# Unequal column tiles in the output product of a convolution and SwiGLU kernel: 384 + 384 and twice 256 + 128 columns

## Chip, cores and metric

The kernel runs on one core of a Trainium2 chip. The metric is the device time of one execution in microseconds (us). All data is float32.

## What is computed

The reference is a lightweight convolution (softmax over seven taps per head, eight heads), followed by RMS normalisation and a SwiGLU feed-forward block:

```
x: (8, 4096, 192)  ->  causal convolution over 7 positions, per head  ->  (32768, 192)
xn  = x / sqrt(mean(x*x) + 1e-6) * rms_g
g   = xn @ w_gate          # 192 x 1536
val = xn @ w_val           # 192 x 1536
out = (g * sigmoid(g) * val) @ w_out      # 1536 x 192, out: (32768, 192)
```

## The kernel before

The 32768 tokens are worked through in 32 pairs of two groups of T = 512 tokens. The first pair runs through a start-up code of its own (`plain`, `outer`); the other 31 are objects of the class `Pair`. For each pair TensorE runs two stages, one after the other:

1. the gate and value products (line L754): 120 matrix products of 64 contraction rows by 512 tokens, by a scheme with fewer products than the plain one, whose sums and differences are made by VectorE, ScalarE and GpSimd;
2. the output product (line L884): hidden values times `w_out`. It too is done by a scheme with seven products of half size in place of eight. The table `OUTS` lists them: each entry has a form (which sum of hidden values, which sum of weights), one of three PSUM banks X, Y, Z in which it accumulates, and a range of steps k. Over a pair that makes 42 steps.

One step multiplies a hidden tile `src` (128 hidden rows by 512 tokens) with 96 columns of weights, `right` (128 hidden rows by three blocks of 32 features). The weights are the stationary operand and the tokens are the moving one, so the result lies with features on partitions and tokens along the row: 96 features by 512 tokens. TensorE is used as four column tiles of 32 columns (`tile_position=(0, 32 i)`), and tile i writes the PSUM partitions 32 i to 32 i + 31. The 96 x 512 results fill 128 partitions by 384 columns of a bank. Before the change all four tiles do the same amount in two products each:

- columns 0 to 255 (`wide`): tiles 0 and 1 have feature block 0, tiles 2 and 3 have block 1; the 32-token blocks go alternately to the even and the odd tile of the two;
- columns 256 to 383 (`slim`): all four tiles have feature block 2, and every fourth 32-token block each.

So a step is eight products, four of 256 columns and then four of 128. `Pair.products` is a generator: it yields after each product of stage 1 and after each half of a step. The order of all other engines' work is a list written out by hand (`ORDER`), where a word like `p2` means that TensorE's generator is taken two yields further, and the other words name an operation and its engine (V VectorE, A ScalarE, G GpSimd, D a DMA). The waits between engines follow from the data.

When a bank is complete, VectorE (L899) transposes it in blocks of 32 x 32 into the output tile `o_sb`, whose partitions are then tokens. There are two output tiles per pair, one per group of 512 tokens, in a pool of two buffers. Each is stored by the words `Dst0-` and `Dst1-` early in the next pair (L957): three DMAs per group before the change, each with runs of 64 features (256 bytes) per token. The DMAs are issued by the sync engine's queue (SP), in the order of the list: the stores of group 0, the loads of the convolution's input xh for a later pair, the stores of group 1, the writes of the normalised activations to a buffer xd in DRAM, and at the end of the pair the loads of xb, the next pair's moving operand, from xd (words `DfetA` and `DfetB`, four DMAs of 384 KB, L659). In the last pair there is no next pair: the stores of group 1 come as soon as its sums are done, those of group 0 end the program, and the middle feature block's stores (c == 1) are issued by ScalarE's queue.

Constants: `P` = 128, `Q` = 32, `NQ` = 4, `HP` = 64, `NM` = 3, so `NM * P` = 384.

Of the kernel before, what the change touches and what calls it, by code (L numbers as in the profile page):

```python
# [19 lines left out]
def kernel(  # L20
# [11 lines left out]
    P = nc.NUM_PARTITIONS  # L32
# [10 lines left out]
    T = 512  # L43
# [3 lines left out]
    HP = P // 2  # L47
    KP = D // HP
    Q = 32
    NQ = P // Q  # L50
# [7 lines left out]
    LOW, UPP = slice(0, HP), slice(HP, P)  # L58
# [178 lines left out]
    def load_out(i):  # L237
# [28 lines left out]
        out=taps[:], in0=w_sb[:], in1=stat[:].to_broadcast([P, H, K]), op=ALU.subtract  # L266
# [7 lines left out]
        out=taps[:], in0=taps[:], in1=ssum[:].to_broadcast([P, H, K]), op=ALU.mult  # L274
# [153 lines left out]
    def part_tap(p, k, j):  # L428
# [4 lines left out]
        if k == 0:  # L433
            h = SIDE[j]
            acc[p, j] = h, pick(h, False)
# [11 lines left out]
        if k == K - 1:  # L447
            h, i = acc.pop((p, j))
            free[h].append(i)
            ended[p] = ended.get(p, 0) + 1  # L450
            if ended[p] == len(SIDE):
                x_sb.pop(p)
# [229 lines left out]
    def pick(h, full):  # L682

        i = next((i for i in free[h] if ((h, i) in whole) == full), free[h][0])
        free[h].remove(i)
        return i
# [5 lines left out]
    def put(at, do):  # L692
        heapq.heappush(line, (at, next(tick), do))
# [10 lines left out]
    def copy(eng, dst, src, s=1):  # L704
        if eng == "A":
            nc.scalar.activation(out=dst, in_=src, func=AF.Copy, scale=float(s))  # L706
        elif s < 0:
            nc.vector.tensor_scalar(out=dst, in0=src, scalar1=-1.0, scalar2=None, op0=ALU.mult)
        else:
            nc.vector.tensor_copy(out=dst, in_=src)  # L710
# [95 lines left out]
    NM = D // (2 * Q)  # L806
# [13 lines left out]
    )  # L820
    HOME = {"X": 0, "Y": 1, "Z": 1}
    SIDE = (0, 1, 0)
    RIGHT = {1: B11, 2: B21, 3: B22, 4: T4, 5: T1, 6: T2, 7: T3}

    class Pair:
# [36 lines left out]
        def products(self):  # L862
            for u, v, i in itertools.chain(*CHAINS):
                for h in range(2):
                    self.units[u].product(h, v, i)
                    yield
            for form, b, lo, hi in OUTS:
                first = form in (1, 7)
                if first:
                    self.open(b, False)  # L870
                for k in range(lo, hi):
                    src, right = self.left(form, k), RIGHT[form][:, k]
                    fresh = first and k == 0
                    wide = src.rearrange("p (b q e) -> p q b e", q=2, e=Q)
                    slim = src.rearrange("p (b q e) -> p q b e", q=NQ, e=Q)
                    for i in range(NQ):
                        self.tile(b, i, 0, 2 * P, right[:, i // 2], wide[:, i % 2], fresh)
                    yield
                    for i in range(NQ):
                        self.tile(b, i, 2 * P, P, right[:, 2], slim[:, i], False)  # L880
                    yield

        def tile(self, b, i, at, n, left, cols, fresh):
# [30 lines left out]
        def do(self, eng, name):  # L914
            act, *at = name.split(".")
            p, n = self.p, NM * P
            if name in self.past:
                return
            self.past.add(name)
            if len(at) == 2:  # L920
                self.units[int(at[1])].do(eng, act, int(at[0]))
            elif at:
                self.sum(int(act[1]), int(at[0]), eng)
            elif act == "c1":
                self.open("Y", True)
                copy(eng, self.some("Y"), self.some("X"))
            elif act in ("s7", "c2"):
                t = self.tl[act] = tiles.pop(0)
                copy(eng, t[:, 0:n], self.some("Z" if act == "s7" else "X"))
            elif act in ("C22", "C21"):  # L930
                t = self.tl["s7" if act == "C22" else "c2"][:, 0:n]
                b = "X" if act == "C22" else "Z"
                nc.vector.tensor_tensor(out=t, in0=self.some(b), in1=t, op=ALU.add)
                if b == "Z":
                    self.close(b)
                    if p == PAIRS - 1:
                        for name in ("T22", "T21", "st1"):
                            if name not in self.past:
                                self.do(eng, name)
            elif act in ("T22", "T21"):  # L940
                t = self.tl.pop("s7" if act == "T22" else "c2")
                self.turn(t, 1, int(act[2]) - 1)
                tiles.append(t)
            elif act in ("T11", "T12"):
                b = "Y" if act == "T11" else "X"
                self.turn(self.bank(b), 0, int(act[2]) - 1)
                self.close(b)
            elif act in ("st0", "st1"):
                g = int(act[2])
                r = p * PT + g * T  # L950
                o = self.o_sb.pop(g)[:].rearrange("p a d -> p (a d)")
                o = o.rearrange("p (b d) -> p b d", d=HP)
                for c, rows, lo, hi in ((0, LOW, 0, 8), (1, UPP, 0, 8), (2, slice(0, P), 8, 12)):
                    n = T // (hi - lo)
                    to = out[r : r + T, c * HP : (c + 1) * HP].rearrange("(b p) d -> p b d", p=n)
                    q = nc.scalar if c == 1 and p == PAIRS - 1 else nc.sync
                    q.dma_start(out=to, in_=o[rows, lo:hi, :])  # L957
            else:
                self.ahead(eng, act)

# [16 lines left out]
    def plain(hts):  # L977


        groups = [(u, g, f) for u in range(NU) for g in (1, 0) for f in range(NF)]  # L980
        groups[0 : 2 * NF] = [(0, g, f) for f in range(NF) for g in (1, 0)]
        held = {}

        def products():
            for u, g, f in groups:
                if len(hts) <= u:
                    hts.append(big.tile([P, 2, NF, T], F32, name="ht"))
                bks = held[u, g, f] = [free[h].pop(0) for h in range(2)]
                for k in range(KP):
                    for h in range(2):  # L990
                        nc.tensor.matmul(  # L991
                            out=bank(h, bks[h])[:], lhsT=wf[u][HALF[h], k * NF + f, :],
                            rhs=xb[HALF[h], g, k, :], start=(k == 0), stop=(k == KP - 1),
                            skip_group_check=True,
                        )
                yield

        def silus():
            for i in groups:
                sg = tiles.pop(0)  # L1000
                nc.scalar.activation(out=sg[:], in_=bank(0, held[i][0])[:], func=AF.Silu)
                held[i].append(sg)
                yield

        def values():
            for u, g, f in groups:
                *bks, sg = held.pop((u, g, f))
                nc.vector.tensor_tensor(  # L1008
                    out=hts[u][:, g, f, :], in0=bank(1, bks[1])[:], in1=sg[:], op=ALU.mult
                )  # L1010
                tiles.append(sg)
                for h in range(2):
                    free[h].append(bks[h])
                yield

        return products(), silus(), values()

    LAG = 138
# [114 lines left out]
    p, sl, v = plain(hts)  # L1133
# [31 lines left out]
    c = base + 200  # L1165
# [4 lines left out]

    for j in range(len(SIDE)):
        put(c + 240 + 700 * (j // 2), functools.partial(part_tap, 2, 0, j))
        for k in range(1, K):
            at = c + 250 + 100 * k + 50 * j if j < 2 else c + 960 + 80 * k
# [58 lines left out]
```

## Time and profile before

| | |
|---|---|
| median of 3 runs | 2621.24 us (2618.13 to 2623.8) |
| profiled execution, its own time | 2620.28 us |
| its span, first to last instruction | 2618.4 us |
| instructions | 71028 |
| TensorE busy | 2580.3 us (99%), 29002 matmul records, granted clock 0.999 |
| VectorE, ScalarE, GpSimd busy | 87%, 62%, 79% |
| DMA | 138.01 MB, mean 53 GB/s |
| instruction packets of queue q8 | 227, 3.72 MB |

How to read it: PE is TensorE's matmul side, PEld its weight loads, DVE is VectorE, ACT ScalarE, POOL GpSimd, SP the sync engine; a q behind an engine's name is its queue of instructions or DMAs. A row of a group gives the line, the engine, the operation, the result and operand by the program's names (`ps` is a PSUM bank, `ht` a hidden tile, `nt`, `early`, `more`, `tls` and `tile` are work tiles, `wo_sb` the output weights, `x` the buffer of the first input tile, which later holds sums of the weights), the shape (`128*32 128x256`: 128 contraction rows, 32 stationary columns, 256 moving columns), the count, the busy time and the mean of one, and the idle time before. An f32 product stands in the trace as two records, each with a weight load. "issue" is time in which an engine waited for nothing that the profile shows.

### The profile page before, as it was taken

The page shows a single profiled execution, that of the slowest core. Times are in us where ns is not written, and L with a number is a line of the kernel's source. Part 1 is how long each engine was busy: PE and PEld are TensorE (multiplying, and loading weights), DVE is VectorE, ACT ScalarE, POOL GpSimd, SP SyncE. Part 2 cuts the span into 40 slices and gives each one's busy share as a digit, 9 for nine tenths or more (in the row PEclk, how much of TensorE's full clock was granted, in tenths as well). Part 3 has the DMA queues.
Part 4 walks back from the last instruction along what each step waited for, and adds up shares of the span by engine and source line. Part 5 has one row for each costly group of instructions (what it writes and reads, how often), then busy time and mean ns, then how long its engine had stood idle before and what let it go on. Part 6 is the DMA issues. An engine that isn't in the chain of part 4 may idle for free.

```text
span 2618.4 us, 71028 instructions
## 1 busy us (share of the span) xinstructions
PE 2580.3 (99%) x29002; PEld 1866.1 (71%) x29002; DVE 2265.0 (87%) x3617; ACT 1617.3 (62%) x2967; POOL 2079.0 (79%) x1693
## 2 busy tenths in 40 slices
PE   6999999999999999999999999999999999999999
PEld 3677777777767777777776777777777777777776
DVE  8888888888888988888888888888898888888875
ACT  5375556765556765557755567655577555676554
POOL 3877788877888777888787887778887778877776
PEclk9999999999999999999999999999999999999999
DMA  6322331323312223213233222233132332222210
GB/s 143 54 47 51 63 53 36 63 39 63 63 36 53 50 51 63 54 35 63 39 63 63 41 48 51 51 63 58 34 59 44 58 63 43 46 57 45 50 38 14
DMA packets 510659, 138.01 MB, mean 53 GB/s; under 512 B 482300, under 2 KB 484860, under 8 KB 510205
## 3 DMA queue, kind: packets, MB, share of 16 engines
q1 hardware_dynamic: 508716, 133.18, 27.2%
q8 instruction: 227, 3.72, 0.6%
q14 instruction: 100, 0.82, 0.1%
q10 hardware_dynamic: 1616, 0.29, 0.1%
HBM read 83.87 MB, written 49.55 MB: 51 GB/s over the span
## 4 chain that ended last, share of the span: by engine, by line
PE 96%; DVE 2%; DMA 1%; issue 0%; POOL 0%; ACT 0%; SPq 0%; DVEq 0%; POOLq 0%; ACTq 0%
PE ps L754 62%; PE ps L884 33%; PE ps L991 1%; PE ps L1031 1%; DMA x<-in_x_dram 0%; DMA xb<-xd 0%; DVE y L405 0%; DVE ht L1008 0%; DVE y L420 0%; DVE y L393 0%; DVE xc L304 0%; PE ps L594 0%; DVE wf L319 0%; ACT xb L614 0%; DVE xc L668 0%
## 5 line engine op out<-in xcount | busy, mean ns | idle before, releaser
L754 PE MATMUL ps<-xc,wf 64*128 64x512 f32 x4960 | 1252.8, 592 | 1.6 <-DVE xc L668 1.1
L754 PEld LDWEIGHTS ps<-xc,wf 64*128 64x128 f32 x4960 | 760.9, 186 | 308.1 <-issue 88.8
L754 PE MATMUL ps<-xb,wf 64*128 64x512 f32 x2480 | 709.1, 589 | 0.0
L706 ACT ACTIVATE tls<-ps 128x512 f32<-128x512 f32 (+1 forms) x636 | 365.7, 589 | 375.5 <-PE ps L884 211.0
L798 POOL TENSOR_TENSOR ht<-ht,tile 128x512 f32<-128x512 f32 x295 | 375.2, 1279 | 272.8 <-ACT tile L791 271.4
L706 ACT ACTIVATE tile<-ps 128x512 f32<-128x512 f32 x697 | 400.1, 594 | 271.2 <-PE ps L754 158.4
L754 PEld LDWEIGHTS ps<-xb,wf 64*128 64x128 f32 x2480 | 392.9, 187 | 141.2 <-issue 38.7
L706 ACT ACTIVATE ps<-ps 128x512 f32<-128x512 f32 (+1 forms) x651 | 366.9, 578 | 54.1 <-PE ps L884 38.9
L912 POOL TENSOR_TENSOR early<-ht 128x512 f32<-128x512 f32 x279 | 379.2, 1364 | 4.9
L444 DVE SCALAR_TENSOR_TENSOR ps<-xh,tp,ps 128x512 f32<-128x512 f32 x450 | 312.1, 745 | 1.7 <-ACT ps L436 0.6
L798 POOL TENSOR_TENSOR ht<-ht,tls 128x512 f32<-128x512 f32 x201 | 255.2, 1276 | 72.4 <-ACT tls L791 70.9
L884 PE MATMUL ps<-ht,wo_sb 128*32 128x256 f32 (+1 forms) x6944 | 310.5, 326 | 0.0
L778 DVE TENSOR_TENSOR tile<-ps,tile 128x512 f32<-128x512 f32 x373 | 255.0, 687 | 56.1 <-PE ps L754 53.5
L884 PEld LDWEIGHTS ps<-ht,wo_sb 128*32 128x32 f32 x6944 | 216.3, 110 | 92.8 <-POOL ht L798 23.5
L884 PE MATMUL ps<-ht,x 128*32 128x256 f32 (+1 forms) x5952 | 250.1, 326 | 0.4 <-issue 0.4
L912 POOL TENSOR_TENSOR ht<-ht 128x512 f32<-128x512 f32 x186 | 248.3, 1350 | 0.0
L791 ACT ACTIVATE tile<-tile 128x512 f32<-128x512 f32 x373 | 233.1, 629 | 12.3 <-DVE tile L778 12.3
L884 PEld LDWEIGHTS ps<-ht,x 128*32 128x32 f32 x5952 | 190.5, 110 | 54.2 <-issue 1.6
L778 DVE TENSOR_TENSOR ht<-ps,tls 128x512 f32<-128x512 f32 x311 | 211.8, 681 | 0.0
L778 DVE TENSOR_TENSOR ht<-ps,tile 128x512 f32<-128x512 f32 x309 | 210.4, 681 | 0.1
L778 DVE TENSOR_TENSOR tls<-ps,tls 128x512 f32<-128x512 f32 x247 | 169.4, 686 | 28.1 <-PE ps L754 26.1
L884 PE MATMUL ps<-early,x 128*32 128x256 f32 (+1 forms) x4464 | 193.5, 326 | 0.0
(129 smaller groups left out, 3132.8 us busy)
## 6 DMA issues: line engine op xcount, KB each, us to landing
xb<-xd SPq DMA_DIRECT2D x124, 384.0 KB
xd<-yn SPq DMA_DIRECT2D x248, 96.0 KB
out_dram<-o_sb SPq DMA_DIRECT2D x184, 128.0 KB
xh<-in_x_dram SPq DMA_DIRECT2D x192, 105.0 KB
xh<-in_x_dram SPq DMA_DIRECT2D x56, 98.4 KB
ht<-in_moe_w_gate_dram SPq DMA_DIRECT2D x12, 192.0 KB
ht<-in_moe_w_val_dram SPq DMA_DIRECT2D x12, 192.0 KB
tls<-in_moe_w_out_dram SPq DMA_DIRECT2D x8, 192.0 KB
```

The lines of the kernel that those rows point to most:

```text
L444: nc.vector.scalar_tensor_tensor(out=dst, in0=xk, scalar=w, in1=at, op0=ALU.mult, op1=ALU.add)
L706: nc.scalar.activation(out=dst, in_=src, func=AF.Copy, scale=float(s))
L754: nc.tensor.matmul(out=self.new(v, h, True) if first else self.old(v, h), lhsT=wf[self.u][HALF[h], WAT[i], :], rhs=x_op(XOP[i])[HALF[h]], ...
L778: nc.vector.tensor_tensor(out=self.hv(v) if h else t[:], in0=self.old(v, h), in1=t[:], op=plus(s))
L791: nc.scalar.activation(out=t[:], in_=src[:], func=AF.Silu)
L798: engine[eng].tensor_tensor(out=self.hv(v), in0=src, in1=t[:], op=ALU.mult)
L884: nc.tensor.matmul(out=self.bank(b)[i * Q : (i + 1) * Q, at : at + n], lhsT=left, rhs=cols, start=fresh, stop=True, skip_group_check=True, ...
L912: engine[eng].tensor_tensor(out=dst, in0=a, in1=b, op=op)
L991: nc.tensor.matmul(out=bank(h, bks[h])[:], lhsT=wf[u][HALF[h], k * NF + f, :], rhs=xb[HALF[h], g, k, :], start=(k == 0), stop=(k == KP - 1 ...
L1031: nc.tensor.matmul(out=bank(h, bks[h])[:, w : w + D], lhsT=hts[f // NF][HALF[h], g, f % NF, j * P : (j + 1) * P], rhs=wo_sb[HALF[h], f, :] ...
```

## The change

A step becomes six products. Tiles 0 and 1 take one product of 384 columns each: feature blocks 0 and 1 for the first 384 tokens. Tiles 2 and 3 take two each: first feature block 2, the even and the odd 32-token blocks (256 columns each), then feature block 0 (tile 2) and 1 (tile 3) for the last 128 tokens. Each tile still streams 384 columns per step. The first yield comes after four products as before, the second after two. Since features and tokens lie in other places of the bank, and so of `o_sb`, a group is stored with five DMAs in place of three: feature block columns 0 to 63 and 64 to 127 in a part of 384 tokens (32 partitions by 12 runs) and one of 128 (32 by 4), and columns 128 to 191 in one (64 by 8).

```
+    WIDE = NM * P
...
-                    wide = src.rearrange("p (b q e) -> p q b e", q=2, e=Q)
-                    slim = src.rearrange("p (b q e) -> p q b e", q=NQ, e=Q)
-                    for i in range(NQ):
-                        self.tile(b, i, 0, 2 * P, right[:, i // 2], wide[:, i % 2], fresh)
+                    two = src.rearrange("p (b q e) -> p q b e", q=2, e=Q)
+                    for i in range(2):
+                        self.tile(b, i, 0, WIDE, right[:, i], src[:, 0:WIDE], fresh)
+                    for i in range(2):
+                        self.tile(b, 2 + i, 0, T // 2, right[:, 2], two[:, i], fresh)
                     yield
-                    for i in range(NQ):
-                        self.tile(b, i, 2 * P, P, right[:, 2], slim[:, i], False)
+                    for i in range(2):
+                        self.tile(b, 2 + i, T // 2, T - WIDE, right[:, i], src[:, WIDE:T], False)
                     yield
...
-                for c, rows, lo, hi in ((0, LOW, 0, 8), (1, UPP, 0, 8), (2, slice(0, P), 8, 12)):
-                    n = T // (hi - lo)
-                    to = out[r : r + T, c * HP : (c + 1) * HP].rearrange("(b p) d -> p b d", p=n)
+                wide, half = WIDE // Q, T // HP
+                for c, i, m, lo, hi, at in (
+                    (0, 0, 1, 0, wide, 0), (1, 1, 1, 0, wide, 0), (2, 2, 2, 0, half, 0),
+                    (0, 2, 1, half, wide, WIDE), (1, 3, 1, half, wide, WIDE),
+                ):
+                    n = m * Q
+                    rows = slice(r + at, r + at + (hi - lo) * n)
+                    to = out[rows, c * HP : (c + 1) * HP].rearrange("(b p) d -> p b d", p=n)
                     q = nc.scalar if c == 1 and p == PAIRS - 1 else nc.sync
-                    q.dma_start(out=to, in_=o[rows, lo:hi, :])
+                    q.dma_start(out=to, in_=o[i * Q : i * Q + n, lo:hi, :])
```

## Prediction

> **What bounds the kernel now.** I read the page first: busy shares, granted clock, the chain that ended last.
>
> ```profile
> span 2618.4 us, 71028 instructions
> PE 2580.3 (99%) x29002; PEld 1866.1 (71%) x29002; DVE 2265.0 (87%) x3617; ACT 1617.3 (62%) x2967; POOL 2079.0 (79%) x1693
> PEclk9999999999999999999999999999999999999999
> ...
> PE 96%; DVE 2%; DMA 1%; issue 0%; POOL 0%; ACT 0%; SPq 0%; DVEq 0%; POOLq 0%; ACTq 0%
> ```
>
> TensorE is the bound, at its full clock. The change touches L884, the output products. Next view, the groups by shape: how many records a step makes and how long each is. (Ends of matmul records are modelled, so I work with their starts.)
>
> ```profile
> L884 PE MATMUL ps<-ht,wo_sb 128*32 128x256 f32 x3472 | 273.6, 380 | 0.0
> L884 PE MATMUL ps<-ht,wo_sb 128*32 128x128 f32 x3472 | 184.9, 273 | 0.0
> ```
>
> All L884 groups together hold 20832 matmul records. A step is eight products, and each f32 product stands as two records: 16 a step, 20832/16 = 1302 steps, 42 in each of 31 pairs. The chain of waits gives the time of a pair's output stage:
>
> ```profile
> 1176.76 52.06 PE ps L754 x240
> 1228.83 27.44 PE ps L884 x672
> ```
>
> 27.44 us for 42 steps is 653 ns. Record by record in an undisturbed stage the four column tiles start 7 ns apart; a 256-column record is followed by its tile's next after 216 ns, a 128-column one after 109 ns: 2 x 216 + 2 x 109 = 650 ns. The columns alone, from the difference of the two forms (107 ns for 128 more), are 2 x 213.3 + 2 x 106.7 = 640 ns. So each record costs its tile 2 to 3 ns, 10 ns a step.
>
> Not every stage takes 27.44 us. The busy times stage by stage:
>
> ```profile
> core 0: us, PE busy (x), PEclk, DMA share, GB/s
> 511.00:539.40 28.40, 27.90 (x673) 1.00 0.25 58
> 591.60:619.00 27.40, 27.40 (x673) 1.00 0.28 60
> 1068.80:1097.10 28.30, 27.77 (x673) 1.00 0.25 58
> 2185.60:2215.00 29.40, 28.03 (x673) 1.00 0.26 57
> ```
>
> Same records, up to 2 us longer, and PE stands still inside. From the first to the last L884 start, 22 of the 31 stages take 27.235 us to within 1 ns, and nine take more: 0.56, 1.11, 0.93, 0.99, 0.82, 0.29, 0.25, 0.18, 1.97; in all 7.1 us. Who held PE? The waits:
>
> ```profile
> PE ps L884 <- issue: 3.3, 5, 1.4
> ```
>
> No engine did. The DMA view of the time before one such stop (524.26 us) says what did:
>
> ```profile
> q1 hardware_dynamic: 809, 1.55, 55.1%
> q8 instruction: 1, 0.02, 0.6%
> ...
> xb<-xd SPq DMA_DIRECT2D x4, 384.0 KB
> ```
>
> That is the window 510 to 522 us. q8 carries TensorE's instructions: 227 packets, 3.72 MB, is 16 KB each, 256 instructions of 64 bytes, and 227 x 256 covers PE's 2 x 29002 loads and matmuls. In those 12 us PE used over 500 instructions and got one packet, because the four loads of xb filled the DMA engines. Counting records up to each packet's start: normally a packet starts when PE is 180 to 200 instructions into a block of 256; before the stops it starts at 330 to 399, PE stops 450 to 460 in, and goes on about 2.7 us after the packet's start. These late packets fall in the stages that lost time, the nine and no other.
>
> **The change part by part.**
>
> *Products.* Per step 12 matmul records and 12 loads in place of 16 and 16. Tiles 0 and 1 each run two records of 384 columns; tiles 2 and 3 each run two of 256 and two of 128. Every tile still streams 384 columns twice over: 640 ns. Tiles 2 and 3 keep the four record gaps they have now, 650 ns. Tiles 0 and 1 fall to about 2 x (320 + 3) = 646 ns, then have to wait for the other two, since whoever reads the bank needs all four. Bounds: if the 10 ns were a shared cost of all 16 records, 12 would cost 7.9 ns: -2.6 ns x 1302 = -3.4 us; if the long tiles set the pace, -4.5 x 1302 = -5.9 us; on the bad side see the first rival. I take 0, by the nearest row: the gap follows the tile's own record (216, 109) whether its neighbours start with it or elsewhere, as after a stop.
>
> Do unequal records run side by side at all? The change stands or falls with it, and one rule speaks against. First the row, the timeline after the stop at 524 us:
>
> ```profile
> 525.39 0.38 PE L884 MATMUL ps<-ht,x 128*32 128x256 f32 x1
> 525.56 0.31 PE L884 MATMUL ps<-nt,x 128*32 128x128 f32 x3
> 525.61 0.38 PE L884 MATMUL ps<-ht,x 128*32 128x256 f32 x1
> 525.67 0.31 PE L884 MATMUL ps<-nt,x 128*32 128x128 f32 x3
> 525.78 0.86 PE L884 MATMUL ps<-ht,x 128*32 128x256 f32 x16
> ```
>
> One tile is a step ahead (operand ht, 256 columns, started at 525.39 and 525.61) while three are at the 128-column records of nt: these start at 525.56 and again at 525.67, before the 256-column record begun at 525.61 can have streamed its 213 ns. In such staggered stages a step still takes 650 ns. The Trainium skill, "TensorE: Matmul & The Clock Gate", section "Part 3: Packing small matmuls", says matmuls keep program order in start and end. By it tile 2's 128-column record could not begin before tile 0's 384-column record has ended: +107 ns a step, +139 us. By the row: 0. I go by the row, which shows both lengths at once, though not 384 beside 256.
>
> *Instructions.* PE issues 24 instead of 32 per 650 ns: 37 per us, not 49. A block lasts 6.9 us, not 5.2. From the normal packet start (185) to the stop (455) are 270 instructions: 5.5 us now, 7.3 us then. A packet needs 2.7 us, so it may be late by 2.8 us now and 4.6 us then. The worst lateness in this execution is (399 - 185)/49 = 4.4 us. So the stops of all nine stages fit inside the new slack, if the packets are delayed by the same time, which the unchanged xb loads suggest. I book -7.1 us and leave 0.3 for a new alignment: -6.8. A rule again: "Runtime: NRT & Kernel Launch", section "Instruction fetch mechanics", holds that fetching is hidden by slower dispatch and a block boundary costs next to nothing. By it fewer instructions bring 0; the stages above lost 7.1 us at block boundaries, so the measurement decides.
>
> *Stores.* Ten per pair for six; bytes and 256-byte runs are the same (384 + 384 + 512 + 128 + 128 runs a group for 3 x 512). Each costs SP about 0.63 us (median of L957): the loads of xh queue 1.3 us later, the xd writes 2.5 us later. Behind them stand the xb loads, which wait 32 us for L754 in a pair (973.7 us in 30 times), so nothing; without that cover it would be 2.5 x 30 = 76 us. What waits for the output tiles is the transpose most of a pair later. The stores start in the L754 stage, away from the xb burst.
>
> *The end.* The last stores are exposed. Now SP and ACT issue at 2613.35, before the second transpose (2613.25 to 2613.52) ends; then both need it: +0.2 us. SP has three to issue instead of two (+0.65 us), the last with 128 runs instead of 512; the 1536 packets after 2614.5 took 2.7 us in either form. Between +0.2 and +1.3 us; I take +0.5.
>
> VectorE, ScalarE and GpSimd keep their instructions; a stall removed makes PE meet them at the places the undisturbed stages show, where nothing is late.
>
> **Sum.** Profiled execution, 2620.3 us (span 2618.4 and 1.9 around it): 2620.3 + 0 - 6.8 + 0.5 = 2614.0. The median of the runs is 2621.2, 1.0 above it: forecast 2615.0, or -0.24%.
>
> **The rivals.**
>
> *Tiles in rounds (slower).* If a short record waits for the long one beside it, a step is 320 + 320 + 107 ns and then the next: +139 us, 2754 us if only the 107 counts. It decides from the point where tile 2's 128-column record starts later than 432 ns into its step. Against it: the timeline above and the 650 ns of staggered stages. For it: no record of 384 exists yet. 0.08. A milder form, 10 ns lost in each step because a long record delays the issue of the short ones (+13 us before the gain, 2628 us), with 0.04.
>
> *The stops stay.* Fewer instructions per block shift where the packets fall, and the burst of loads could catch them as before; then only the stores remain: 2621.7. For: lateness comes from the DMA burst, which stays. Against: the slack arithmetic. 0.17.
>
> *Cheaper records too.* If the 10 ns a step are shared: 2611.6, down to 2609 by the longer bound. For: 25% fewer loads. Against: gaps follow the tile. 0.14.
>
> *Forecast,* stops gone, steps as before: 0.57.
>
> **How the numbers follow.** About 0.2% (5 us) is what a measurement of this kernel can tell from no change. The forecast and the cheap-record case are faster, but the forecast lies only 1 us past that bound and the runs spread over 6 us, so 0.07 of it goes to within; the stops-stay case is within; rounds and their milder form are slower. Faster 0.50 + 0.14 = 0.64, same 0.17 + 0.07 = 0.24, slower 0.12. Range: 2607 (both gains, and the 2 us by which the runs lie to either side) to 2622 (stops stay); outside lie the 0.12 of the slower cases and the tails of the others.
>
> **What would show it.** Right: 15624 L884 matmul records; stages at 27.4 us, nearly all alike; issue before L884 under 0.5 us; about 186 q8 packets; tile starts of 323, 216 and 109 ns. Wrong: undisturbed stages longer than 27.6 us (tiles hinder one another) or shorter than 27.3 (records cost PE as a whole), stops of 0.5 us and more at late q8 packets, or SP waits that move into the xb loads.

## The result, and the profile after

| | before | changed |
|---|---|---|
| median of 9 runs | 2620.19 us (2617.59 to 2623.94) | 2613.14 us (2612.04 to 2615.56) |
| ratio to the kernel before | | 0.9974, 95% interval 0.9964 to 0.9984 |
| profiled execution, its own time | 2620.28 us | 2612.71 us |
| its span | 2618.4 us | 2610.6 us |

The changed kernel is 7 us (0.26%) faster; 2615.0 was forecast, in a range of 2607 to 2622. The page of the changed kernel (L884 is now L886, the stores' L957 is L964):

```profile
span 2610.6 us, 60706 instructions
PE 2576.8 (99%) x23794; PEld 1872.7 (72%) x23794; DVE 2272.0 (87%) x3617; ACT 1617.1 (62%) x2967; POOL 2078.9 (80%) x1693
...
q8 instruction: 186, 3.05, 0.5%
```

5208 matmul records are gone and 41 packets of TensorE's instructions with them. TensorE is still the bound. Now the same busy times stage by stage (PE busy, records, clock, DMA share), in which four stages of the kernel before showed 27.4 to 29.4 us:

```profile
core 0: us, PE busy (x), PEclk, DMA share, GB/s
509.80:537.20 27.40, 27.40 (x505) 1.00 0.24 60
589.30:616.70 27.40, 27.40 (x505) 1.00 0.25 60
1066.50:1093.90 27.40, 27.40 (x505) 1.00 0.25 60
2179.90:2207.30 27.40, 27.40 (x505) 1.00 0.27 60
```

All alike, and PE busy from end to end. From the first to the last L886 start every one of the 31 stages takes 27.234 or 27.235 us, the very time of an undisturbed stage before. The chain of waits agrees with that: the output stage of a pair keeps its 27.44 us, with fewer records.

```profile
430.16 27.44 PE ps L886 x337
457.60 52.34 PE ps L754 x237
509.94 27.44 PE ps L886 x337
```

(x337 is close to the 42 x 8 = 336 records of tiles 2 and 3; the stage has 504.) The waits of PE no longer have a row for the output product:

```profile
PE ps L533 <- ACT early L401: 17.9, 2, 17.2
PE ps L594 <- ACT xc L587: 5.6, 1, 5.6
PE ps L1038 <- POOL wo_sb L311: 2.5, 2, 1.4
```

What is left is the start of the program. Does the burst of xb loads still hold up the packets? It does, most of all in the output stage that begins at 350.6 us. Its DMA view of 356.5 to 364 us:

```profile
q1 hardware_dynamic: 418, 0.79, 44.8%
q8 instruction: 1, 0.02, 1.0%
...
xb<-xd SPq DMA_DIRECT2D x2, 384.0 KB
```

The one packet starts at 363.5 us, 7.8 us after the packet before it, where a block lasts 6.9. Counted as in the prediction (loads, matmuls and the sequencer's instructions of PE in order of their start), it starts 306 instructions into its block of 256, and at 37 instructions per us that is (306 - 185)/37 = 3.3 us late, more than the 2.8 us reckoned for the kernel before. PE runs on.

That packet is the only one of its kind. In the kernel before, 11 packets in nine output stages start more than 2.8 us late, and those are the nine that stop; in the changed kernel it is this one, and the mean lateness over all packets of output stages is 0.15 us for 0.78. In the stage at 509.8 us, which lost 1.1 us before, the packets now start 161 to 172 instructions into their blocks, which is on time. In none of the nine stages that had stopped does a packet now start later than 241 instructions into its block, an estimated (241 - 185)/37 = 1.5 us late. So in the profiled execution the larger slack was needed once, in a stage that had not stopped before; in the nine the packets were no longer late enough to stop either kernel.

The difference of the two spans (7.85 us) is made up of three parts: 7.10 us of stops in nine output stages are gone; from the last L88x start to the end it is 5.71 us instead of 5.88; and the first output stage starts 0.58 us earlier, at 191.32 instead of 191.90 us, in code that the change does not touch. Among the seven other kernels below, this start lies anywhere between 190.3 and 193.0 us, so it is taken as scatter.

### The profile page after: what moved, and what is told of

Same layout as the page of the kernel before. It is cut to its first block, busy times and chain, and to the rows that moved or that the text cites. A ratio compares the mean times of both kernels' runs of the same rounds, so it can differ in the third digit from the quotient of the medians.

```text
span 2610.6 us, 60706 instructions
## 1 busy us (share of the span) xinstructions
PE 2576.8 (99%) x23794; PEld 1872.7 (72%) x23794; DVE 2272.0 (87%) x3617; ACT 1617.1 (62%) x2967; POOL 2078.9 (80%) x1693
## 4 chain that ended last, share of the span: by engine, by line
PE 96%; DVE 2%; DMA 1%; POOL 0%; issue 0%; ACT 0%; SPq 0%; DVEq 0%; POOLq 0%; ACTq 0%
PE ps L754 62%; PE ps L886 33%; PE ps L998 1%; PE ps L1038 0%; DMA x<-in_x_dram 0%; DMA xb<-xd 0%; DVE y L405 0%; DVE y L420 0%; DVE ht L1015 0%; DVE y L393 0%; DVE xc L304 0%; PE ps L594 0%; DVE wf L319 0%; ACT xb L614 0%; DVE xc L668 0%
## 5 line engine op out<-in xcount | busy, mean ns | idle before, releaser
L754 PE MATMUL ps<-xc,wf 64*128 64x512 f32 x4960 | 1252.5, 592 | 0.8 <-DVE o_sb L1050 0.3
L754 PEld LDWEIGHTS ps<-xc,wf 64*128 64x128 f32 x4960 | 759.9, 186 | 308.4 <-issue 85.9
L754 PE MATMUL ps<-xb,wf 64*128 64x512 f32 x2480 | 708.9, 589 | 0.0
L754 PEld LDWEIGHTS ps<-xb,wf 64*128 64x128 f32 x2480 | 392.5, 187 | 141.4 <-issue 37.7
L886 PE MATMUL ps<-ht,wo_sb 128*32 128x128 f32 (+2 forms) x5208 | 318.6, 380 | 0.0
L886 PEld LDWEIGHTS ps<-ht,wo_sb 128*32 128x32 f32 x5208 | 234.1, 110 | 81.5 <-POOL ht L798 23.5
L886 PE MATMUL ps<-ht,x 128*32 128x128 f32 (+2 forms) x4464 | 250.7, 379 | 0.0
L886 PEld LDWEIGHTS ps<-ht,x 128*32 128x32 f32 x4464 | 184.6, 110 | 61.2
L886 PE MATMUL ps<-early,x 128*32 128x256 f32 (+2 forms) x3348 | 196.0, 379 | 0.0
```

What stands on the lines that cost most here:

```text
L754: nc.tensor.matmul(out=self.new(v, h, True) if first else self.old(v, h), lhsT=wf[self.u][HALF[h], WAT[i], :], rhs=x_op(XOP[i])[HALF[h]], ...
L886: nc.tensor.matmul(out=self.bank(b)[i * Q : (i + 1) * Q, at : at + n], lhsT=left, rhs=cols, start=fresh, stop=True, skip_group_check=True, ...
```

## Experiments

Theory: the gain is the stops alone; TensorE's instruction packets come late in the xb burst, and fewer instructions per step let it bear that. Rivals: the uneven tiles or the layout bring the gain; the stops belong to something else than the DMA; records cost TensorE as a whole.

### The count put back, the layout kept

```
-                        self.tile(b, i, 0, WIDE, right[:, i], src[:, 0:WIDE], fresh)
+                        self.tile(b, i, 0, T // 2, right[:, i], src[:, 0 : T // 2], fresh)
...
+                    for i in range(2):
+                        self.tile(b, i, T // 2, P, right[:, i], src[:, T // 2 : WIDE], False)
```

> The changed kernel with its layout and its ten stores, but each 384-column product of tiles 0 and 1 cut into 256 + 128: eight products and 32 TensorE instructions a step again. Theory (late instruction packets): the stops of up to 2 us before L886 come back in about nine of the 31 output stages, 227 packets on q8, undisturbed stages still 27.235 us; about 2620 us, ratio to the kernel before 0.999 to 1.001. Rival (the uneven tiles and the layout bring the gain, not the count): stays at 2613, ratio 0.997, all stages 27.235 us.

Measured 2621.43 us, ratio 1.0000 (0.9992 to 1.0009). The profile has stops in ten stages, 6.99 us in all, undisturbed stages of 27.235 us, and the waits show the row again:

```profile
PE ps L888 <- issue: 2.7, 6, 0.8
```

The layout, its ten stores and the place of tokens and features are those of the changed kernel; with 32 instructions a step the gain is gone, and ten packets are again more than 2.8 us late. The number of products did it.

### The burst halved, the products of before

```
-        for rows in (LOW, UPP):
+        for rows in (LOW,):          # in fetch_part, the loads of xb
```

> The kernel before, with the xb loads of the pairs from the third on cut to partitions 0 to 63 (the other half of xb is not loaded, so that half of the product's input is stale). 32 instructions a step as before. Theory (the packets are late because the xb burst fills the DMA engines): with the burst halved packets start at most about 60 instructions late, under the slack, and the stops go without any change in the products: about 2613 us, ratio 0.997, all 31 stages 27.235 us. Rival (the stops belong to the 32-instruction steps themselves, whatever the DMA does): nine stages still lose about 7 us in all, 2620 us, ratio 1.000. DVE may also start its sums a little earlier, which TensorE should not feel.

Measured 2613.57 us, ratio 0.9972 (0.9961 to 0.9983): the whole gain of the change, without it. One stage of 31 lost 0.44 us, at a packet that started 334 instructions into its block.

```profile
PE ps L884 <- issue: 0.2, 1, 0.2
```

Only this packet is more than 2.8 us late, for 11 with the whole burst. So the stops come from the DMA burst of the xb loads.

### Half as many instructions again

```
-                    for i in range(NQ):
-                        self.tile(b, i, 0, 2 * P, right[:, i // 2], wide[:, i % 2], fresh)
+                    for c in range(2):
+                        for i in range(NQ):
+                            cols = wide[:, i % 2][:, c * NQ : (c + 1) * NQ]
+                            self.tile(b, i, c * P, P, right[:, i // 2], cols, fresh and c == 0)
```

> The kernel before with every 256-column product cut in two: twelve products of 128 columns a step, 48 TensorE instructions. Theory: two effects apart. The records: six gaps a tile instead of four, 6 x 109 = 654 ns a step, undisturbed stages 27.4 us, +5 us over 1302 steps. The packets: a block lasts 3.5 us, the slack from packet start to stop falls from 5.5 to 3.7 us, of which 2.7 are needed; the xb burst makes packets late in nearly every pair, 1 to 3 us of stops each: +30 to +100 us, 2650 to 2720 us, ratio 1.012 to 1.038. Rival (no shortage of instructions): only the records, 2625 us, ratio 1.002.

Measured 2766.2 us, ratio 1.0558 (1.0538 to 1.0579): more than the theory's range. The records cost what was said: an undisturbed step takes 655 ns, 4.5 ns more, 5.9 us over all. The rest was underestimated. All 31 stages stop, and together they are 148.5 us longer than 31 undisturbed stages of before, so 142.6 us remain beside the records. They have two parts. The waits and a stretch of the timeline show the stops:

```profile
PE ps L886 <- issue: 95.6, 61, 4.2
```

```profile
1128.82 1.27 PE L886 MATMUL ps<-ht,wo_sb 128*32 128x128 f32 x40
1132.88 0.75 PE L886 MATMUL ps<-ht,wo_sb 128*32 128x128 f32 x20 [2.79 <-issue]
```

The other part is the clock. In 13 of the 31 stages, each time within 0.8 us of the end of a stop of about 2.5 us or more, the granted clock falls to a half for 3.41 us (mean over the execution 0.989, before 0.999). Such a stretch, and the time right after it:

```profile
core 0: us, PE busy (x), PEclk, DMA share, GB/s
206.50:209.70 3.20, 3.20 (x69) 0.50 0.02 5
210.00:213.20 3.20, 3.20 (x128) 1.00 0.02 5
```

At half clock about half as many records run in the same time. That costs at most 13 x 3.41/2 = 22 us, which leaves 120 us or more for the stops, about 4 us a pair where 1 to 3 were reckoned. The loss at half clock was in no reckoning.

At 73 instructions per us the slack is an estimated 270/73 - 2.7 = 1.0 us. A stage has two bursts, one for each pair of xb loads, and in the timeline's stage a long stop follows each of them, at 1124.4 and at 1129.8 us. 18 packets start 449 instructions into a block, just before PE runs dry at about 455, and then PE stands until the packet is of use, nearly 3 us later. Whether one late packet makes the next one late, or each burst does it anew, is not shown.

### Ten stores, the products of before

```
-                for c, rows, lo, hi in ((0, LOW, 0, 8), (1, UPP, 0, 8), (2, slice(0, P), 8, 12)):
+                for c, rows, lo, hi in (
+                    (0, LOW, 0, 6), (1, UPP, 0, 6), (2, slice(0, P), 8, 12),
+                    (0, LOW, 6, 8), (1, UPP, 6, 8),
+                ):
```

> The kernel before with its products, but ten stores per pair in place of six (the stores of feature columns 0 to 63 and 64 to 127 are cut into 6 + 2 blocks). Theory (SP has 30 us to spare in a pair): no change but in the last microseconds, 0 to +1.3 us at the end of the program, ratio 0.999 to 1.001, stops as before. Rival (stores delay the xd writes and xb loads): SP's wait before the xb loads vanishes, PE waits at L754, +2 us a pair, +60 us.

Measured 2621.15 us, ratio 1.0001 (0.9993 to 1.0009). Stops in 11 stages, 7.8 us; from the last L884 start to the end 6.09 us, 0.2 more than before. A cost of the stores cannot be told from none, and they do not touch the stops.

### Every tile with two records

```
-                        self.tile(b, 2 + i, 0, T // 2, right[:, 2], two[:, i], fresh)
+                        self.tile(b, 2 + i, 0, WIDE, right[:, 2], src[:, i * P : i * P + WIDE], fresh)
...
-                    for i in range(2):
-                        self.tile(b, 2 + i, T // 2, T - WIDE, right[:, i], src[:, WIDE:T], False)
```

> The changed kernel with four products of 384 columns a step, one for each column tile: tiles 2 and 3 take the third feature block for tokens 0 to 383 and 128 to 511 and leave out the 128-column products of the other two blocks, so the sums of part of the tokens are incomplete. Each tile still streams 384 columns, in two records instead of four. Theory (a record's gap belongs to its own tile, and tiles 2 and 3 with four records set the step): a step takes 645 ns instead of 650, as tiles 0 and 1 already show in the changed kernel; stages 27.0 us, -5.3 ns x 1302 = -7 us against the changed kernel: 2606 us, ratio to the kernel before 0.9945. Rival (the gap is a cost of the step or of the issue as a whole, or the long tiles only look faster): 650 ns a step, 2613 us, ratio 0.997.

Measured 2605.53 us, ratio 0.9941 (0.9927 to 0.9954), no stops. The chain of its output stage, beside the 27.44 us of the changed kernel:

```profile
269.84 27.23 PE ps L884 x336
376.63 52.06 PE ps L754 x240
428.70 27.23 PE ps L884 x336
```

0.21 us less in 42 steps is 5 ns a step, 6.5 us over 31 pairs. Both kernels stream the same 384 columns per tile and step; only tiles 2 and 3 lost two of their four records. The rival of a cost shared by all records would also have shortened the step when the change took its TensorE instructions from 32 to 24, and that left it at 650 ns. So the gap of a record belongs to its tile, and the tile with most records sets the step. The starts in the changed kernel show the same from the other side: in the stage at 1066.57 us tiles 0 and 1 start a record every 322.5 ns, 645 ns a step, while tiles 2 and 3 need 650; tiles 0 and 1 run away from the others by 5 ns a step and end the stage about 0.2 us early, which brings nothing.

### A longer burst, at 24 and at 32 instructions a step

Behind the second pair of xb loads, in the changed kernel and then in the kernel before:

```
+        if g == 0:
+            for i in range(4):
+                to, half = junk[i // 2], slice(i % 2 * T, (i % 2 + 1) * T)
+                nc.sync.dma_start(out=to[:, half], in_=xd[:, half])
```

> The changed kernel with four more DMAs of 384 KB (2 KB runs, copies of xd inside DRAM that nothing reads) behind the second pair of xb loads: the burst in the output stage becomes about twice as long. Products, order and TensorE instructions are those of the changed kernel. Theory (late packets): 24 instructions a step bear a packet up to 4.6 us late; a backlog of about 10 us makes packets later than that, so stops before L886 come back, 1 to 4 us in most pairs: +20 to +100 us, ratio 1.005 to 1.035. Rival (the change removed the stops because shorter instruction streams do not depend on the DMA at all): 2613 us, ratio 0.997. If VectorE's sums or the xb loads are late instead, PE waits at L754 and not at L886.

Measured 2613.61 us, ratio 0.9969 (0.9957 to 0.9981): no stop in any stage. The theory's number missed. The burst was longer, as the DMA view of 1231 to 1243 us shows, but no packet was much later for it: the latest start is 311 instructions into a block, 3.4 us late, inside the slack of 4.6.

```profile
q1 hardware_dynamic: 1250, 2.36, 63.0%
q8 instruction: 2, 0.03, 1.2%
...
junk<-xd SPq DMA_DIRECT2D x4, 384.0 KB
```

More packets are late, but the latest is hardly later: 11 packets in ten stages start 2.8 to 3.4 us late (289 to 311 instructions into a block), for one in the changed kernel. This left open whether the extra DMAs had tested anything, so they went into the kernel before as well:

> The kernel before with the same four extra DMAs of 384 KB behind the second pair of xb loads as in e6_burst, where 24 instructions a step bore them without a stop (packets started there at most 311 instructions into a block, 3.4 us late). Theory (a packet may be 2.8 us late at 32 instructions a step, 4.6 us at 24): here the same DMAs make stops, in more stages than the nine of the kernel before and up to 1.5 us each: +3 to +25 us against before, ratio 1.001 to 1.010. Rival (the extra DMAs do not delay the packets, so e6_burst said nothing on the slack): 7 us of stops as before, ratio 0.999 to 1.001.

Measured 2626.03 us against 2620.12 in the same session, ratio 1.0023 (1.0017 to 1.0030). Stops in 23 of 31 stages, 12.2 us where the kernel before has 7.1:

```profile
PE ps L889 <- issue: 4.9, 9, 1.1
```

(The waits count only the time in which no modelled matmul runs, so they show less than the stages lose.) 25 packets in 23 stages are more than 2.8 us late. The same DMAs cost the 32-instruction step 6 us and the 24-instruction step nothing, though there too packets in ten stages were later than 2.8 us. That is the slack, seen from the DMA's side.

## Why the prediction was right, point by point

- *Stops, booked at -6.8 us.* Right in size: -7.10 us in the profile. The 0.3 us kept for a new alignment was not needed. That the number of instructions is the cause is shown by the first experiment, and that the xb burst makes the packets late by the second. The slack is shown by the two kernels with a longer burst: at 24 instructions a step packets up to 3.4 us late stop nothing, at 32 those from about 2.8 us on do. Where between 3.4 us and the reckoned 4.6 the limit at 24 lies was not reached.
- *"If the packets are delayed by the same time".* This did not hold, and it erred to the safe side: one packet was more than 2.8 us late in place of 11. The prediction reckoned with more slack for the same lateness; in the profiled execution the nine stops went because the packets came less late, and the slack was needed in one other stage. That the sum came out right is to this extent luck. The lower lateness goes with the number of instructions, since the kernel with the same layout and eight products has ten such packets. Why fewer and larger instructions bring packets that are less late stays open.
- *Products, booked at 0.* Right: 27.235 us in every stage, 650 ns a step. Tiles 0 and 1 run at 645 ns (646 was reckoned), tiles 2 and 3 set the pace. The bounds of -3.4 and -5.9 us were not reached: the gap is per tile, as the experiment with two records shows.
- *Rounds.* The rival fell: the 128-column records of tiles 2 and 3 run beside the 384-column ones at no loss. The rule that the prediction cites from the Trainium skill ("TensorE: Matmul & The Clock Gate", Part 3: matmuls keep program order in start and end) does not hold across column tiles, for the starts at least: at the end of the stage at 1066.57 us the first 384-column record of the last step starts 26.47 us into it, and a 128-column record of the step before that only at 26.58 us. (Ends are modelled in the trace, so it says nothing on them.) The milder form fell with it: a step takes 650 ns, as before.
- *The stops stay.* This rival fell; with eight products in the new layout the stops do stay, 6.99 us of them.
- *Instruction fetching hidden.* The rule cited from the Trainium skill ("Runtime: NRT & Kernel Launch") would have made the gain 0; 7 us at 32 instructions a step and about 120 us at 48 say that for TensorE in this stage it does not hold.
- *Stores, 0 in the pairs.* Right, by the experiment with ten stores. SP's wait for L754 before the xb loads took up the delay: it fell from 973.7 to 924.2 us in 30 times, 1.7 us a pair.
- *The end, booked at +0.5 us.* Wrong in size, and perhaps in sign: the tail came out 0.17 us shorter. The store issues do start later after the last record (1.00 us for 0.82), as reckoned. What was mis-sized is what follows: SP's first issue takes 0.36 us where about 0.63 was reckoned for each, the first data packet starts 0.83 us after that issue for 1.25 before, and the last ends at 3.20 us for 3.84. The kernel with eight products and the same stores shows the same (0.83 and 3.26 us, tail 5.84 us), the one with the other cut of ten stores does not (1.25 and 3.70 us, tail 6.09 us). So the cut of the stores makes their start faster; that the whole tail is shorter, 5.71 and 5.84 us for 5.88, is within what single executions can scatter by.
- *The sum.* 2614.0 was reckoned for the profiled execution, 2612.7 came: 0.3 from the stops, 0.7 from the end, 0.6 from the scatter of the start, less 0.3 around the span. Of the 1.9 us by which the median of the runs lies under the forecast, 1.0 us is that the kernel before had 2620.19 us in the nine runs, and not 2621.24.

## What to carry to other kernels

In a stage that one engine bounds, list the stage's repetitions: equal work with unequal times is a stop, or a stretch at a lower clock. "issue" as its releaser, during a DMA burst, suggests that the engine ran out of instructions. To check that, count how far into its block the engine is when each packet starts, in the stages that stop and in those that do not; the number of packets in a window depends too much on where the window is laid. In this kernel both fewer, larger instructions and a shorter burst gave the time back, and the instructions per microsecond told how late a packet may be. Where column tiles run unequal records, count the records of the tile that has most; taking records from the others moved nothing here.

## What was not expected of the hardware

Lateness does not add up with the length of the burst: with four more DMAs behind the second pair of loads a packet started at most 3.4 us late, for 3.3. And a stop can cost more than its own time: at 48 instructions a step, 13 of the stops came with 3.41 us of half clock.
